# Narrow idle products at the front of TensorE, and a new hand-written order behind them

## The chip, the cores and the metric

The kernel runs on one core of a Trainium2 chip. The metric is the device time of one execution in microseconds (us). TensorE (PE) multiplies, VectorE (DVE) and ScalarE (ACT) do elementwise work, GpSimd (POOL) issues the loads, SyncE (SP) issues the stores. All engines run their own instruction streams in a fixed order and wait for each other by semaphores.

## The reference

Attention with a sliding window of 64 tokens over 8 batches, 8 heads, 576 tokens and head size 64, then a two-layer block with SiLU between the layers:

```
scores = scale * q @ k.T ; mask = (0 <= i - j) & (i - j < 64)
attn = softmax(where(mask, scores, -1e9)) ; a = attn @ v
x = a as (4608 tokens, 512)
h = x @ w_in            # 512 x 2048
out = (h * sigmoid(h)) @ w_out   # 2048 x 512, float32
```

## The kernel before

**Tiles.** The 4608 tokens go in nine tiles of 512 (eight blocks of 64 tokens each). For each tile a "visit" makes the attention of its blocks, for heads 0-3 and for heads 4-7 apart. A visit is: scores on PE (L292; for the very first visits a mask is added by products with `ident`, L285), four exponentials on ACT (L307), a mask product on DVE (L314, not for the first visits), the values product on PE (L323), a reciprocal and a scaling on DVE (L334, L338), and a block transpose on DVE into `xt`, the tile of x (L442). Then come the two layers on PE. Tile 0 does them plainly (L450 and L464, SiLU at L461). Tiles 1 to 8 use a seven-product scheme for 2x2 blocks (L507 and L519), with sums of weights (`wsum`, L469) and of tokens (`xsum`, L485/L487; `gsum`, L493/L496) on DVE, joins on DVE (L526) and copies on ACT (L523).

**The first tile.** It is visited in two halves of 256 tokens. I call the four groups A1 and A2 (heads 0-3, first and second 256 tokens) and B1 and B2 (heads 4-7). Their scores stand on PE in the order A1, A2, B1, B2, their values in the order A1, B1, A2, B2. Each group's scores need q and k of its four heads, loaded by POOL (L224, one load for q and one for k of four heads) and turned by DVE (L255 for k, L258 for q). Values need v, loaded by POOL (L235) and copied half a tile up or down by DVE or ACT (L273, L275). The first layer begins with eight "half products" (4 matmuls each), which use the first 256 tokens alone: four of them read the rows of `xt` from heads 0-3, four those from heads 4-7.

**What sets the order.** `Plan.run` walks the table `ORDER`. A word such as `166P2506` says that step 166 goes to PE and takes the PSUM banks 2, 5, 0 and 6; the letters A, D, G and S stand for ACT, DVE, POOL and SP. So the table fixes the order on each engine, which of ACT and DVE does a copy, and the order in which POOL issues its loads. Eight POOL loads can be under way at a time, and their data come in the order of issue.

**Idle products.** `warm` (L895) multiplies a tile of zeros, `fill`, into a PSUM bank that nobody reads. The plan makes 90 such steps (67 to 156), each 512 columns wide. Of these the table places 36: 24 before the first scores, 7 between A2's and B1's scores, 4 between B2's scores and A1's values, and 1 among the first half products. Steps of this kind that the table doesn't place are left out.

Of the kernel before, what the change touches and what calls it, by code (L numbers as in the profile page):

```python
# [29 lines left out]
class Plan:  # L30
# [88 lines left out]
def kernel(ctx, tc, q, k, v, w_in, w_out, out):  # L119
# [774 lines left out]
    def warm(op_bank):  # L894
        nc.tensor.matmul(banks[op_bank.idx][:, 0:FILL], lhsT=fill[:, 0:128], rhs=fill[:, 0:FILL], start=True, stop=True)  # L895
# [92 lines left out]
```

## Time and profile before

| | us |
|---|---|
| median of 3 runs | 277.21 |
| lowest, highest | 275.41, 277.24 |
| the profiled execution | 276.81 |
| its span, first to last instruction | 275.0 |
| PE busy in the span | 264.7 |
| DVE, ACT, POOL busy | 214.0, 195.6, 129.7 |

The span is what the instruction records cover; the 1.8 us between it and the profiled execution's own time lie around the records and take no part in the argument. PE is busy nearly all the time, but its idle products count as busy too. The DMA engines are close to full until about 185 us.

### The profile page before, as it was taken

The page shows a single profiled execution, that of the slowest core. Times are in us where ns is not written, and L with a number is a line of the kernel's source. Part 1 is how long each engine was busy: PE and PEld are TensorE (multiplying, and loading weights), DVE is VectorE, ACT ScalarE, POOL GpSimd, SP SyncE. Part 2 cuts the span into 40 slices and gives each one's busy share as a digit, 9 for nine tenths or more (in the row PEclk, how much of TensorE's full clock was granted, in tenths as well). Part 3 has the DMA queues.
Part 4 walks back from the last instruction along what each step waited for, and adds up shares of the span by engine and source line. Part 5 has one row for each costly group of instructions (what it writes and reads, how often), then busy time and mean ns, then how long its engine had stood idle before and what let it go on. Part 6 is the DMA issues. An engine that isn't in the chain of part 4 may idle for free.

```text
span 275.0 us, 10018 instructions
## 1 busy us (share of the span) xinstructions
PE 264.7 (96%) x4335; PEld 218.0 (79%) x4342; DVE 214.0 (78%) x426; ACT 195.6 (71%) x361; POOL 129.7 (47%) x194
## 2 busy tenths in 40 slices
PE   7978999999999999999999999999999999999993
PEld 2557844688888888888888888888888888888882
DVE  3757578999996898889799999988867967824741
ACT  1555993699749993987499958893888489537910
POOL 7944566988959758596387335940000000000000
PEclk9999999999999999999999999999999999999999
DMA  6999999999999959999979998990400040003004
GB/s 106 167 190 210 198 191 172 144 198 157 118 151 209 127 56 97 242 122 87 93 179 159 83 126 122 136 121 2 155 0 2 6 155 0 2 29 127 0 2 157
DMA packets 101631, 31.62 MB, mean 115 GB/s; under 512 B 92368, under 2 KB 95440, under 8 KB 101584
## 3 DMA queue, kind: packets, MB, share of 16 engines
q0 software_dynamic: 96128, 21.51, 86.1%
q1 hardware_dynamic: 5456, 9.44, 9.7%
q8 instruction: 35, 0.57, 0.9%
q14 instruction: 12, 0.10, 0.1%
HBM read 42.99 MB, written 9.44 MB: 191 GB/s over the span
## 4 chain that ended last, share of the span: by engine, by line
PE 88%; ACT 4%; DVE 4%; issue 1%; ACTq 0%
PE room L519 36%; PE room L507 35%; PE room L292 4%; PE room L323 4%; PE room L450 4%; PE room L895 4%; PE room L464 2%; ACT es L307 2%; DVE o L338 1%; ACT L307 1%; ACT g L461 1%; DVE es L314 1%; DVE xt L442 1%; PE room L285 1%; ACT L461 0%
## 5 line engine op out<-in xcount | busy, mean ns | idle before, releaser
L529 ACT ACTIVATE g<-room 128x512 bf16<-128x512 f32 x96 | 53.6, 605 | 4.5 <-PE room L507 4.1
L507 PEld LDWEIGHTS <-wsum 128*128 128x128 bf16 x512 | 49.9, 98 | 7.2 <-issue 1.0
L519 PEld LDWEIGHTS <-gsum 128*128 128x128 bf16 x512 | 49.1, 98 | 6.2 <-DVE gsum L496 0.2
L507 PE MATMUL room<-xsum,wsum 128*128 128x256 bf16 x384 | 53.3, 272 | 0.5 <-ACT es L307 0.3
L307 ACT ACTIVATE es<-room 128x512 bf16<-128x512 f32 (+1 forms) x88 | 39.1, 533 | 14.2 <-PE room L292 9.6
L519 PE MATMUL room<-wsum,gsum 128*128 128x256 bf16 x384 | 48.4, 273 | 0.0
L507 PEld LDWEIGHTS <-w_in_sb 128*128 128x128 bf16 x384 | 37.2, 98 | 4.7
L519 PEld LDWEIGHTS <-g 128*128 128x128 bf16 x384 | 36.7, 98 | 4.6
L526 DVE TENSOR_TENSOR room<-room,part 128x512 f32<-128x512 f32 (+1 forms) x41 | 27.8, 684 | 13.7 <-ACT part L523 3.5
L227 POOL DMA_DIRECT2D nat<-in_k_dram x48 | 30.0, 631 | 15.1 <-DVE kT L265 11.4
L507 PE MATMUL room<-xt,w_in_sb 128*128 128x256 bf16 x256 | 36.8, 273 | 0.0
L519 PE MATMUL room<-w_out_sb,g 128*128 128x256 bf16 x256 | 35.7, 273 | 0.0
L227 POOL DMA_DIRECT2D nat<-in_q_dram x48 | 29.9, 637 | 9.7 <-DVE qT L268 6.1
L523 ACT COPY ot<-room 128x512 f32<-128x512 f32 (+1 forms) x23 | 13.3, 582 | 28.6 <-PE room L519 21.5
L235 POOL DMA_DIRECT2D vv<-in_v_dram x32 | 29.6, 940 | 5.0 <-DMA nat<-in_k_dram 1.7
L523 ACT COPY room<-room 128x512 f32<-128x512 f32 x40 | 23.3, 592 | 12.1 <-PE room L507 10.8
L526 DVE TENSOR_TENSOR fin<-room,part 128x512 f32<-128x512 f32 x32 | 21.6, 683 | 9.0 <-PE room L507 6.1
L523 ACT COPY part<-room 128x512 f32<-128x512 f32 x40 | 23.6, 598 | 6.4 <-PE room L519 3.2
L241 POOL DMA_DIRECT2D vv<-in_v_dram x24 | 22.3, 934 | 12.0 <-PE room L323 11.5
L314 DVE TENSOR_TENSOR es<-es,strip 128x1024 bf16<-128x1024 bf16 (+1 forms) x36 | 21.9, 626 | 6.7 <-ACT es L307 6.4
L338 DVE TENSOR_TENSOR o<-room,recips 128x896 bf16<-128x896 f32 (+2 forms) x36 | 25.9, 726 | 0.8
L496 DVE TENSOR_TENSOR gsum<-g,gsum 128x512 bf16<-128x512 bf16 x64 | 25.1, 415 | 0.4
(75 smaller groups left out, 376.8 us busy)
## 6 DMA issues: line engine op xcount, KB each, us to landing
out_dram<-ot SPq DMA_DIRECT2D x16, 512.0 KB, 3.9
vv<-in_v_dram POOLq DMA_DIRECT2D x56, 128.0 KB, 5.0
nat<-in_k_dram POOLq DMA_DIRECT2D x48, 72.0 KB, 4.0
nat<-in_q_dram POOLq DMA_DIRECT2D x48, 72.0 KB, 3.7
w_in_sb<-in_moe_w_in_dram POOLq DMA_DIRECT2D x8, 256.0 KB, 9.2
w_out_sb<-in_moe_w_out_dram POOLq DMA_DIRECT2D x8, 256.0 KB, 9.0
nat<-in_k_dram POOLq DMA_DIRECT2D x4, 288.0 KB, 8.0
nat<-in_q_dram POOLq DMA_DIRECT2D x4, 288.0 KB, 8.2
```

Of the source, the lines that this page charges most:

```text
L227: queue[e].dma_start(out=nats[b % 2][a][kk][32 * h:32 * h + 32].rearrange("p (n x) -> p n x", n=NB), in_=(q, k)[kk][b, 4 * a + h].rearrang ...
L235: queue[e].dma_start(out=vv[b % 2][:, :, 2 * g + 1, 0:D], in_=v[b, :, 128 * g:128 * g + 128].rearrange("h p d -> p h d"))
L241: queue[e].dma_start(out=vv[b % 2][:, :, 2 * g, 0:D], in_=v[b, :, 128 * g - 64:128 * g + 64].rearrange("h p d -> p h d"))
L307: nc.scalar.activation(out=es_part(a, blocks)[:, h], in_=banks[bank.idx][:, 0:64 * n], func=ACTF.Exp, scale=scale)
L314: nc.vector.tensor_mul(t, t, strip[:, s:s + n].rearrange("k n i -> k (n i)").unsqueeze(1).to_broadcast([128, 2, 64 * n]))
L338: nc.vector.tensor_mul(out, at_values(bank, n)[:, :, :, 0:D], recips[:, w:w + 2 * n].rearrange("k (t n) -> k t n", t=bank.wide).unsqueeze( ...
L496: nc.vector.tensor_sub(out=dst[2 * i - 1], in0=g(1, 2 - i), in1=dst[i - 1])
L507: nc.tensor.matmul(banks[bank.idx][:, 256 * i:256 * i + 256], lhsT=lhs(z, i), rhs=rhs(z), start=(start and i == 0 and z == 0), stop=(z == ...
L519: nc.tensor.matmul(banks[bank.idx][:, 256 * m:256 * m + 256], lhsT=lhs(m, i), rhs=rhs(i), start=(start and i == 0 and m == 0), stop=(stop ...
L523: copies[e](out=dst, in_=src)
L526: nc.vector.tensor_add(out=dst, in0=bank, in1=part)
L529: nc.scalar.activation(out=g_tile(pair, 256 * t, 256 * t + 256), in_=src.rearrange("k (f t) -> k f t", f=2), func=ACTF.Silu)
```

## The change

The plan gets 48 further idle steps (1643 to 1690) of 128 columns, and `warm` gets the width as an argument. The table `ORDER` is replaced as a whole. In the new table 17 wide and 19 narrow idle products stand in front of the first scores, mostly in turn, and none anywhere else: the 12 wide ones behind A2's scores are left out. All real steps of the old table stand in the new one, but their order differs on PE, DVE, ACT and POOL through the whole program, and 13 copies change between DVE and ACT (6 go from DVE to ACT, 7 from ACT to DVE).

```
-    "1D 9G 2D 74P7 3D 11G 69P2 72P5 13G 67P0 15G 68P1 73P6 5G 70P3 71P4 19G 7D 78P3 81P6 82P7 86P3 6G 10D 77P2 89P6 90P7 75P0 17G 76P1 80P5 12D 83P0 79P4 "
+    "1D 11G 3D 1643P7 81P6 9G 2D 1644P7 80P5 1645P7 71P4 15G 1646P7 78P3 1647P7 17G 1648P7 89P6 1649P7 1650P7 5G 79P4 1651P7 77P2 1652P7 75P0 6G 1653P7 7D "
...
-    def warm(op_bank):
-        nc.tensor.matmul(banks[op_bank.idx][:, 0:FILL], lhsT=fill[:, 0:128], rhs=fill[:, 0:FILL], start=True, stop=True)
+    def warm(op_bank, n):
+        nc.tensor.matmul(banks[op_bank.idx][:, 0:n], lhsT=fill[:, 0:128], rhs=fill[:, 0:n], start=True, stop=True)
...
-        p.add({"PE": 0.427 * FILL / 512 if i < 4096 / FILL else 0.235 * FILL / 512}, lambda _, wb=wb: warm(wb), [c_fill], 1e6 + i, take=[wb], give=[wb], gate=lambda: first_moe[0]["at"] is None, tag="fill", ins=2)
+        p.add({"PE": 0.427 * FILL / 512 if i < 4096 / FILL else 0.235 * FILL / 512}, lambda _, wb=wb: warm(wb, FILL), [c_fill], 1e6 + i, take=[wb], give=[wb], gate=lambda: first_moe[0]["at"] is None, tag="fill", ins=2)
...
+    for i in range(48):
+        wb = Bank("part")
+        p.add({"PE": 0.107 if i < 32 else 0.06}, lambda _, wb=wb: warm(wb, 128), [c_fill], 2e6 + i, take=[wb], give=[wb], gate=lambda: first_moe[0]["at"] is None, tag="fill", ins=2)
     p.run(ORDER)
```

POOL at its start, before: `nat_87` and `nat_89` are the k of heads 0-3 and 4-7, `nat_86` and `nat_88` their q, `strip` is the mask.

```order
L224 DMA nat_87<-in_k_dram 128x1152
L224 DMA nat_86<-in_q_dram 128x1152
L224 DMA nat_89<-in_k_dram 128x1152
L224 DMA nat_88<-in_q_dram 128x1152
L184 MEMSET strip 128x64
L185 ISA
L185 AFFINE_SELECT strip<-strip 128x64
L187 AFFINE_SELECT strip<-strip 128x64
L235 DMA vv_98<-in_v_dram 128x8x64
```

And POOL at its start now:

```order
L224 DMA nat_86<-in_q_dram 128x1152
L224 DMA nat_87<-in_k_dram 128x1152
L224 DMA nat_88<-in_q_dram 128x1152
L235 DMA vv_98<-in_v_dram 128x8x64
L184 MEMSET strip 128x64
L185 ISA
L185 AFFINE_SELECT strip<-strip 128x64
L187 AFFINE_SELECT strip<-strip 128x64
L191 MEMSET ident 128x128
L192 AFFINE_SELECT ident<-ident 128x128
L193 AFFINE_SELECT ident<-ident 128x128
L224 DMA nat_89<-in_k_dram 128x1152
```

The k of heads 4-7 moved from the third place among the loads to the fifth, behind the first load of v and behind the making of the mask and the identity.

DVE from the first write into `xt_75` (tile 0 of x) to the last, before: `o_100` holds the attention of heads 0-3, `o_101` that of heads 4-7.

```order
L442 STREAM_TRANSPOSE xt_75<-o_100 128x4x2x32
L334 RECIPROCAL recips<-room 128x8
L338 TENSOR_TENSOR o_101<-room,recips 128x2x256
L442 STREAM_TRANSPOSE xt_75<-o_101 128x4x2x32
L945 MEMSET good 128x1
L334 RECIPROCAL recips<-room 128x8 x2
L338 TENSOR_TENSOR o_100<-room,recips 128x2x256
L442 STREAM_TRANSPOSE xt_75<-o_100 128x4x2x32
L338 TENSOR_TENSOR o_101<-room,recips 128x2x256
L442 STREAM_TRANSPOSE xt_75<-o_101 128x4x2x32
```

And now:

```order
L442 STREAM_TRANSPOSE xt_75<-o_100 128x4x2x32
L273 COPY vv_98<-vv_98 64x8x64
L334 RECIPROCAL recips<-room 128x8
L338 TENSOR_TENSOR o_101<-room,recips 128x2x256
L334 RECIPROCAL recips<-room 128x8
L442 STREAM_TRANSPOSE xt_75<-o_101 128x4x2x32
L334 RECIPROCAL recips<-room 128x8
L338 TENSOR_TENSOR o_101<-room,recips 128x2x256
L338 TENSOR_TENSOR o_100<-room,recips 128x2x256
L442 STREAM_TRANSPOSE xt_75<-o_101 128x4x2x32
L442 STREAM_TRANSPOSE xt_75<-o_100 128x4x2x32
```

A copy of v came in from ACT, and of the second halves heads 4-7 (B2) are now turned ahead of heads 0-3 (A2).

118 rows, old and new, of the table ORDER are left out of this document.

## The prediction

> **What bounds the kernel now.** I read the page first, then the busy time by stretches, then the timeline of each engine over the first 32 us.
>
> ```profile
> span 275.0 us, 10018 instructions
> PE 264.7 (96%) x4335; PEld 218.0 (79%) x4342; DVE 214.0 (78%) x426; ACT 195.6 (71%) x361; POOL 129.7 (47%) x194
> PE room L519 36%; PE room L507 35%; PE room L292 4%; PE room L323 4%; PE room L450 4%; PE room L895 4%; PE room L464 2%; ACT es L307 2%; DVE o L338 1%; ACT L307 1%; ACT g L461 1%; DVE es L314 1%; DVE xt L442 1%; PE room L285 1%; ACT L461 0%
> ```
>
> The chain of waits is PE's second and first layers (L519, L507) for seven tenths of the span. The stretches show where PE is not full (start and end, length, then each engine's busy us):
>
> ```profile
> 17.20:22.40 5.20, 4.23 (x109) 3.25 (x110) 3.84 (x10) 1.44 (x3) 2.33 (x4) 1.00 1.22 209
> 34.10:52.40 18.30, 17.31 (x287) 8.37 (x291) 15.26 (x39) 11.86 (x26) 12.81 (x21) 1.00 1.43 163
> 52.40:60.00 7.60, 7.60 (x70) 6.61 (x69) 7.57 (x16) 7.57 (x15) 6.76 (x11) 1.00 1.36 212
> 60.00:270.00 210.00, 209.31 (x3518) 182.59 (x3516) 170.84 (x330) 157.17 (x284) 88.04 (x124) 1.00 0.89 97
> 270.00:275.00 5.00, 0.36 (x4) 0.08 (x1) 0.65 (x1) 0.37 (x1) 0.00 (x0) 1.00 0.38 125
> ```
>
> From 60 to 270 us PE is idle for 0.7 us in 210. The real products are the same in both kernels, so this stretch can hardly shrink, and the time is set by when PE becomes full and by the 5 us of end. What there is to win lies ahead of 52 us. PE's timeline there (start, length, work, and in brackets the idle time before it):
>
> ```profile
> 1.39 7.60 PE L895 MATMUL room<-fill 128*128 128x512 bf16 x24 [1.39 <-DVE fill L213]
> 8.82 0.60 PE L285 MATMUL room<-block,ident 128*128 128x256 bf16 x4
> ...
> 10.60 1.79 PE L895 MATMUL room<-fill 128*128 128x512 bf16 x6
> 12.23 0.60 PE L285 MATMUL room<-block,ident 128*128 128x256 bf16 x4
> ...
> 13.10 0.61 PE L285 MATMUL room<-block,ident 128*128 128x256 bf16 x4
> ...
> 14.00 1.04 PE L895 MATMUL room<-fill 128*128 128x512 bf16 x4
> 14.96 0.67 PE L323 MATMUL room<-vv,es 128*32 128x65 bf16 x44
> 17.21 0.60 PE L323 MATMUL room<-vv,es 128*32 128x65 bf16 x52 [1.58 <-issue]
> 17.74 1.26 PE L450 MATMUL room<-xt,w_in_sb 128*128 128x256 bf16 x8
> 18.93 0.43 PE L323 MATMUL room<-vv,es 128*32 128x65 bf16 x32
> ...
> 21.32 0.60 PE L450 MATMUL room<-xt,w_in_sb 128*128 128x256 bf16 x4 [0.43 <-DVE xt L442]
> 22.42 7.91 PE L450 MATMUL room<-xt,w_in_sb 128*128 128x256 bf16 x71 [0.51 <-DVE xt L442]
> ```
>
> Three holes stand here that no idle product fills: 1.58 us in the middle of B1's values, for which the profile shows no releaser, and 0.43 and 0.51 us for writes into `xt`.
>
> **The change, part by part.** All sums are against the profiled execution, 276.81 us with a span of 275.0. It lies 0.40 under the median of the three runs, 277.21, and inside their spread.
>
> *1. The narrow products at the front.* The wide ones by their two speeds:
>
> ```profile
> 1.39:5.97 4.58, 4.58 (x11) 1.63 (x12) 1.00 0.72 122
> 5.97:8.82 2.85, 2.85 (x14) 1.18 (x12) 1.00 1.09 196
> ```
>
> Eleven take 4.58 us (0.42 each), the other thirteen 2.85 (0.22 each): the clock doubles at about 6 us. Now it is 17 x 512 + 19 x 128 = 11136 columns for 24 x 512 = 12288. The first 4.58 us pass 11 x 512 = 5632 columns; the other 5504 at 0.22 per 512 need 2.4, so the products end at 8.4 instead of 8.82. If each of the 12 further weight loads (0.1 us by the rows above, 1.18 / 12) came on top, they would end at 9.6. The first scores also need q and k turned:
>
> ```profile
> 7.06 1.21 DVE L258 STREAM_TRANSPOSE qT<-nat 128x576 f32<-128x576 f32 x1 [0.22 <-DMA nat<-in_q_dram]
> 8.48 1.26 DVE L255 STREAM_TRANSPOSE kT<-nat 128x576 f32<-128x576 f32 x1 [0.21 <-DMA nat<-in_k_dram]
> 11.86 0.29 DVE L273 COPY vv<-vv 64x512 bf16<-64x512 bf16 x1 [0.74 <-DMA vv<-in_v_dram]
> ```
>
> A1's pair is turned by 8.27. I take 8.4 for A1's start, and 0.4 us sooner for A1 and A2. Nothing of it reaches B1, as the next part shows.
>
> *2. Twelve products left out, k of heads 4-7 later, ACT in another order.*
>
> ```profile
> 9.83 2.32 ACT L307 ACTIVATE es<-room 128x256 bf16<-128x256 f32 x8 [7.61 <-PE room L292]
> 12.17 0.62 ACT L273 COPY vv<-vv 64x512 bf16<-64x512 bf16 x1
> 12.80 0.62 ACT L275 COPY vv<-vv 64x512 bf16<-64x512 bf16 x1
> 13.32 2.29 ACT L307 ACTIVATE es<-room 128x256 bf16<-128x256 f32 x8
> 15.64 0.62 ACT L273 COPY vv<-vv 64x512 bf16<-64x512 bf16 x1
> ```
>
> Eleven of the twelve lie beside these exponentials: B1's scores take over banks of A1 and A2, which come free at 12.15, and began at 12.23. Leaving the seven out gains under 0.1 us. Now ACT begins with an exponential of A2, so at 8.4 + 1.8 = 10.2 (A1 and A2 together took 8.82 to 10.60). B1 waits for seven of them, 0.29 each: 12.3. Its k now lands fifth: the third load was down at 8.46 (its turn began at 8.48), a load of v takes about 1.0 (by the copy at 11.86, which waited for the second of them, behind a fourth load down at about 9.9), one of k or q 1.4 (7.06 to 8.48), so 10.9, and it is turned by 12.2. So B1 starts at 12.4 with no idle products before it, where it started at 12.23 with them.
>
> B2's scores now wait for the last exponential of A2, which stands behind the first of B1: 13.3 + 2 x 0.3 = 13.9 (before 13.10). A1's values follow B2's scores, 0.9 us later, at 14.9; they began at 14.96. So the four left out there gain nothing. The last exponential that B1's values need comes after eight steps of ACT from 13.35, seven exponentials and one copy: 16.0. ACT's last v copy ends at 16.0 + 2 x 0.29 + 0.62 = 17.2, which lets A2's values start at 17.3; they ran right behind the hole that ends at 17.21. Sum of this part: 0.0, bounds -0.3 and +0.8 (if k lands after another load).
>
> *3. The hole at 15.6.* Its row has no releaser. PE's instructions come by DMA:
>
> ```profile
> q8 instruction: 35, 0.57, 0.9%
> ```
>
> 0.57 MB in 35 packets are 16 KB each. PE's 4335 + 4342 instructions share them, 66 bytes each, so a packet holds some 250. Before the hole stand 35 idle products, 144 of scores and 44 of values, with a weight load each: 446 instructions, while the loads keep the DMA engines full. I read the hole as PE waiting for its next instructions. [...]
>
> 36 idle products stand ahead of B1's values now, so the hole stays at that place. I let it end 0.4 us sooner, as the instructions behind A1 begin 0.4 sooner: 16.8. B1's values end near 17.1 (before, their reciprocal began at 17.67). By part 2 A2's values start at 17.3 anyway, so this gains no time of PE, but DVE starts B1's reciprocal at 17.2.
>
> *4. The waits for `xt` and the idle product among the half products.* DVE:
>
> ```profile
> 17.67 0.21 DVE L334 RECIPROCAL recips<-room 128x8 f32<-128x8 f32 x1 [0.68 <-PE room L323]
> 17.91 0.73 DVE L338 TENSOR_TENSOR o<-room,recips 128x512 bf16<-128x512 f32 x1
> 18.68 0.45 DVE L442 STREAM_TRANSPOSE xt<-o 128x256 f32<-128x256 f32 x1
> ...
> 20.82 0.45 DVE L442 STREAM_TRANSPOSE xt<-o 128x256 f32<-128x256 f32 x1 [0.55 <-PE room L450]
> 21.19 0.70 DVE L338 TENSOR_TENSOR o<-room,recips 128x512 bf16<-128x512 f32 x1
> 21.92 0.45 DVE L442 STREAM_TRANSPOSE xt<-o 128x256 f32<-128x256 f32 x1
> ```
>
> A2's turn waited for PE (0.55), and then half products waited for it, though they read other columns: a write into `xt` and the half products around it in the table wait for each other if they share rows of x. So the order decides. Now DVE does: copy 0.3, reciprocal and scaling of B1, reciprocal of A2, turn of B1, reciprocal and scaling of B2, scaling of A2, turn of B2, turn of A2. From 17.2, with 0.2, 0.7 and 0.45 per step: B1 turned at 18.8, B2 at 20.85, A2 at 21.3. On PE from 17.3: two values groups (0.43 each) and eight half products of four matmuls, 7.91 / 71 = 0.11 each, so 0.87 + 3.5 us. The sixth reads rows of heads 4-7 and stands behind B2's turn: it would start at 20.4 and waits until 20.9, 0.4 us. The eight end at 22.1. Before, 25 of their 32 matmuls were done at 22.42, the rest by 22.42 + 7 x 0.11 = 23.2. **Gain 1.1 us**, made of the two waits (0.94) and the idle product (0.22) against a new wait of 0.4 and an earlier start by a quarter of a microsecond. If the hole ends as late as before, DVE is 0.4 later and the gain 0.7; with no wait it is 1.5.
>
> *5. From there to 60 us.* The loads come in the same number and at the same pace, DVE and ACT have the same work but for copies that change sides. In 52.4 to 60 DVE is full, 7.57 of 7.60: a lead of PE alone would end there. DVE's chain starts from tile 1's values, which PE makes, so most of the lead passes on. I keep 1.0 of 1.1, bounds 0 and 1.5 + 1.0 (all the idle time of 34 to 52, 18.30 - 17.31, gone too).
>
> *6. The rest, 60 to 270 us.* The waits of PE there:
>
> ```profile
> PE room L507 <- ACT es L307: 0.3, 1, 0.3
> PE room L323 <- DVE o L338: 0.2, 1, 0.2
> PE room L507 <- issue: 0.2, 1, 0.2
> ```
>
> At most 0.7 can be won. The order is new on all engines and its waits are in no trace. The nearest rows are these 0.3 and 0.2 per wait: two more, half offset by those that go, cost 0.2; that is what I take. The far end is such a wait in each of 14 large visits, 14 x 0.3 = 4.2. The end behind 270 us keeps its stores: 0.
>
> Sum: 276.81 - 1.0 + 0.2 = **276.0 us**.
>
> **The rivals.**
>
> *A: the lead is lost in the stretch where DVE is full*, and nothing else changes: 276.81 + 0.2 = 277.0. For it speaks 7.57 of 7.60; against it that DVE's steps are fed by PE.
>
> *B: the clock falls back.* Without the twelve products PE does 4 x 0.9 us of scores and 0.4 of values from 8.4 to 16.0 and nothing else. If it slows down, it needs again the 4.58 us of work that the front took, at half speed: 4.58 / 2 = 2.3 us lost behind 17.3, and 276.0 + 2.3 = 278.3, slower than before. It decides from the first idle stretch that is long enough. In this trace 1.58 us idle did not do it: the matmuls behind ran at 0.11. My longest stretch is 2.1 us (10.2 to 12.3). [...]
>
> *C: the new order waits in the steady part*: exponentials that free a score bank too late for PE, once in each of 14 large visits, 0.3 each: 276.0 + 4.2 = 280.2, slower. It decides at three such waits, where the gain is gone. For it: DVE is busy for 170.84 and ACT for 157.17 of the 210 us, so a step that moves has little room. Against it: before has one.
>
> *D: the holes go altogether*: the instruction hole (1.58), both waits (0.94) and the idle product (0.22) vanish: 276.81 - 2.74 = 274.1. Against it the exponentials of part 2 and the full DMA engines. [...]
>
> *E: the change does nothing*: the idle products were never on the path, and the rest cancels: 276.8.
>
> **How the numbers follow.** About 1% is what a measurement of this kernel can tell from no change: 274.4 to 280.0 around the median. Forecast 0.42, A 0.13, E 0.07, B 0.10, C 0.17, D 0.11. Of B all but a tenth of its mass stays inside 1%; of C, whose waits may be longer than 0.3, I count everything above; unnamed mishaps of the new order take some of the forecast's mass, 0.05. So slower by over 1%: 0.17 + 0.01 + 0.05 = 0.23; faster by over 1%: D and a little, 0.12; same 0.65. The range leaves out a tenth on each side: 274.3 to 280.3.
>
> **What would show it.** In the new profile: L895 once at the front, ending near 8.4; the second L285 group near 12.4 and B1's values with a hole of about 0.8 us marked "issue"; one wait of L450 on `xt`, not two, and the eight half products done at 22.1; PE full from 52 us on as before, with 0.7 to 1.2 us idle between 60 and 270. Matmuls of 0.22 us at L450 would mean B. Many rows "L507 <- es" or "L519 <- DVE" would mean C. No "issue" row near 16 us would mean D. The forecast is wrong if the first layer's start doesn't move, or if PE idles over 3 us behind 60 us.

## The result and the profile after

The changed kernel took 278.81 us (median of nine runs, 277.76 to 279.10), the kernel before 277.06 beside it (nine runs, 275.41 to 278.29): a ratio of 1.0061, interval 1.0038 to 1.0083. A gain of 0.3% was forecast and a loss of 0.6% came. The loss is smaller than the 1% named in the prediction, but the interval leaves no doubt of its sign. Ratios and intervals here leave out the few runs that the chip made in a slower state, and they are not simply quotients of the medians.

The profiled execution took 278.73 us, 1.92 more than that of before. Its page: the span, the engines' busy time, PE's granted clock in 40 slices, and the chain of waits:

```profile
span 277.0 us, 10005 instructions
...
PE 263.5 (95%) x4337; PEld 218.8 (79%) x4342; DVE 213.3 (77%) x427; ACT 193.8 (70%) x360; POOL 129.6 (47%) x194
...
PEclk9959999999999999999999999999999999999998
...
PE room L519 35%; PE room L507 35%; PE room L450 6%; PE room L464 5%; PE room L292 4%; PE room L323 4%; DMA nat<-in_k_dram 2%; ACT es L307 1%; DVE o L338 1%; POOL nat L224 1%; DVE es L314 0%; DVE kT L255 0%; ACT ot L523 0%; POOL vv L235 0%;
```

Two things are new. PE's granted clock has a 5 in the third of 40 slices, and the load of k stands in the chain. PE's timeline of the front shows both (start, length, work, and in brackets the idle time before it):

```profile
1.39 6.48 PE L895 MATMUL room<-fill 128*128 128x128 bf16 x36 [1.39 <-DVE fill L213]
7.70 0.60 PE L285 MATMUL room<-block,ident 128*128 128x256 bf16 x4
...
10.50 0.54 PE L285 MATMUL room<-block,ident 128*128 128x256 bf16 x2 [0.76 <-ACT es L307]
11.32 0.27 PE L285 MATMUL room<-block,ident 128*128 128x256 bf16 x1 [0.28 <-ACT es L307]
11.88 0.27 PE L285 MATMUL room<-block,ident 128*128 128x256 bf16 x1 [0.28 <-ACT es L307]
13.39 0.42 PE L292 MATMUL room<-qT,kT 32*128 32x64 bf16 x32 [1.24 <-DVE kT L255]
...
15.43 0.68 PE L323 MATMUL room<-vv,es 128*32 128x65 bf16 x34
16.58 0.62 PE L323 MATMUL room<-vv,es 128*32 128x65 bf16 x30 [0.47 <-ACT es L307]
18.02 0.63 PE L323 MATMUL room<-vv,es 128*32 128x65 bf16 x32 [0.81 <-DVE vv L273]
18.58 1.03 PE L450 MATMUL room<-xt,w_in_sb 128*128 128x256 bf16 x4
19.55 0.63 PE L323 MATMUL room<-vv,es 128*32 128x65 bf16 x32
20.11 10.98 PE L450 MATMUL room<-xt,w_in_sb 128*128 128x256 bf16 x92
```

The first row of L450 is the forecast's own test for rival B: four matmuls of the half products take 1.03 us where four of before took 0.60. The same rows show that the hole without a releaser has gone from B1's values (the 30 matmuls at 16.58 wait for exponentials), and that none of the half products waits for `xt`.

The clock changes of the trace lie 3.41 us, or a multiple of it, apart: here at 4.64, 14.88 and 21.70. So I cut the busy time into these stretches (start and end, length, PE, weight loads, DVE, ACT, POOL, the granted clock, DMA share, GB/s):

```profile
4.64:8.05 3.41, 3.41 (x27) 1.99 (x25) 2.57 (x4) 0.00 (x0) 3.26 (x7) 1.00 1.16 193
8.05:11.46 3.41, 2.23 (x74) 1.29 (x72) 1.84 (x4) 1.67 (x7) 3.41 (x6) 1.00 1.68 159
11.46:14.88 3.42, 1.46 (x38) 0.61 (x37) 2.44 (x6) 1.39 (x6) 2.27 (x4) 1.00 1.61 152
14.88:18.29 3.41, 2.12 (x120) 1.71 (x123) 2.01 (x7) 3.34 (x9) 1.96 (x3) 0.50 1.31 201
18.29:21.70 3.41, 3.41 (x71) 2.25 (x60) 2.52 (x6) 0.71 (x1) 1.11 (x2) 0.50 1.23 206
```

After a stretch in which PE was busy for 1.46 of 3.42 us the clock halves, and it comes back after one that PE filled. There was no idle stretch of 3.41 us; the longest single wait behind the first scores is 1.24.

The steady part in the same view:

```profile
60.00:270.00 210.00, 208.97 (x3515) 182.51 (x3513) 171.08 (x329) 155.34 (x283) 87.60 (x123) 1.00 0.88 95
```

PE is busy for 208.97 us there, against 209.31. At the end of the program, the five stores (L533: least, median and longest ns, then first and last start). Of before:

```profile
L533 SPq DMA_DIRECT2D out_dram<-ot x5: 345/418/691, 267.8 to 271.5; - x5
```

And of the changed kernel:

```profile
L533 SPq DMA_DIRECT2D out_dram<-ot x5: 372/421/544, 271.1 to 273.1; - x5
```

PE's last products, of before and then of after:

```profile
269.76 0.60 PE L519 MATMUL room<-w_out_sb,gsum 128*128 128x256 bf16 x4
```

```profile
270.41 0.60 PE L519 MATMUL room<-w_out_sb,gsum 128*128 128x256 bf16 x4
```

PE ends at 270.36 before and 271.01 now. From there to the end of the span it was 4.7 us and is 5.9. So of the 1.92 us about 1.3 lie behind PE's last product and 0.65 ahead of it. Matching the products of the two traces one by one splits the 0.65: PE is 0.75 us behind when the half products are done, only 0.31 behind by 52 us, and 0.8 behind again by 90 us, after this row and a wait of 0.36 us for a copy at 83.67:

```profile
80.86 0.59 PE L292 MATMUL room<-qT,kT 32*128 32x64 bf16 x53 [0.36 <-issue]
```

So there were three suspects: the end, the clock, and a hole at 80 us.

### The profile page after: what moved, and what is told of

It reads as the page before. It is cut to its first block, busy times and chain, and to the rows that moved or that the text cites. A ratio compares the mean times of both kernels' runs of the same rounds, so it can differ in the third digit from the quotient of the medians.

```text
span 277.0 us, 10005 instructions
## 1 busy us (share of the span) xinstructions
PE 263.5 (95%) x4337; PEld 218.8 (79%) x4342; DVE 213.3 (77%) x427; ACT 193.8 (70%) x360; POOL 129.6 (47%) x194
## 4 chain that ended last, share of the span: by engine, by line
PE 89%; DMA 2%; DVE 2%; ACT 2%; POOL 1%; issue 1%; ACTq 0%; DVEq 0%; POOLq 0%
PE room L519 35%; PE room L507 35%; PE room L450 6%; PE room L464 5%; PE room L292 4%; PE room L323 4%; DMA nat<-in_k_dram 2%; ACT es L307 1%; DVE o L338 1%; POOL nat L224 1%; DVE es L314 0%; DVE kT L255 0%; ACT ot L523 0%; POOL vv L235 0%; ACT room L523 0%
## 5 line engine op out<-in xcount | busy, mean ns | idle before, releaser
L235 POOL DMA_DIRECT2D vv<-in_v_dram x32 | 29.4, 928 | 13.9 <-PE room L507 9.6
L523 ACT COPY part<-room 128x512 f32<-128x512 f32 x40 | 23.7, 599 | 7.5 <-PE room L507 4.3
L338 DVE TENSOR_TENSOR o<-room,recips 128x128 bf16<-128x128 f32 (+2 forms) x36 | 25.8, 727 | 0.7
L493 DVE TENSOR_TENSOR gsum<-g 128x1024 bf16<-128x1024 bf16 x32 | 21.6, 684 | 3.5 <-ACT g L529 3.4
```

The costliest lines, as they stand in the source:

```text
L235: queue[e].dma_start(out=vv[b % 2][:, :, 2 * g + 1, 0:D], in_=v[b, :, 128 * g:128 * g + 128].rearrange("h p d -> p h d"))
L338: nc.vector.tensor_mul(out, at_values(bank, n)[:, :, :, 0:D], recips[:, w:w + 2 * n].rearrange("k (t n) -> k t n", t=bank.wide).unsqueeze( ...
L493: nc.vector.tensor_sub(out=gsum[:, u, 0:4:2], in0=gall[:, lo:hi + 1, :, 256:512], in1=gall[:, lo].rearrange("k f (t n) -> k t f n", t=2))
L523: copies[e](out=dst, in_=src)
```

## The experiments

Three series, each on one chip with its own runs of the kernel before, whose medians there were 276.22, 276.50 and 276.65. "PE's end" and "clock halved for" are from the profiled execution of each, the second from the first full clock to PE's end; for the kernel before they were 270.36 and 0.

| kernel | median | ratio and interval | PE's end | clock halved for |
|---|---|---|---|---|
| changed, copy 1627 earlier (`t1_copy`) | 277.93 | 1.0064 (1.0043 to 1.0085) | 271.74 | 10.2 us |
| changed, end of before (`t2_tail`) | 277.52 | 1.0075 (1.0045 to 1.0105) | 270.89 | 10.2 us |
| changed, 17 wide idle products added (`c1_fills`) | 278.61 | 1.0094 (1.0064 to 1.0124) | 271.70 | 0 |
| the same with the end of before (`c2_both`) | 277.81 | 1.0074 (1.0046 to 1.0101) | 271.08 | 0 |
| before, idle products as changed (`b1_edit`) | 276.80 | 1.0031 (1.0005 to 1.0056) | 269.84 | 6.8 us |
| before, the twelve left out (`b1_nofill`) | 277.80 | 1.0022 (0.9990 to 1.0054) | 273.08 | 6.8 us |
| before, end as changed (`b2_tail`) | 278.08 | 1.0051 (1.0023 to 1.0079) | 272.59 | 3.4 us |
| changed, idle products and end of before (`c3_wide`) | 276.63 | 1.0015 (0.9991 to 1.0040) | 269.72 | 0 |
| changed kernel again (`after2`) | 279.31 | 1.0100 (1.0063 to 1.0137) | 272.21 | 10.2 us |
| changed, idle products of before (`c3_late`) | 277.73 | 1.0048 (1.0029 to 1.0067) | 270.10 | 0 |
| `c3_wide` again (`c3_again`) | 276.39 | 1.0003 (0.9977 to 1.0030) | 269.23 | 0 |
| before, narrow front and six of the twelve (`b4_six`) | 276.70 | 1.0015 (0.9994 to 1.0037) | 270.40 | 3.4 us |

### The end: the copy or the place of the stores

```
-1607P 1619P 1616P 1623P 1624P 1625P 1617P 1626P 1629A 1620P 1627A 1628D
+1607P 1627A 1619P 1616P 1623P 1624P 1625P 1617P 1626P 1629A 1620P 1628D
```

> The changed kernel, with one step of ACT moved: the output copy 1627, ready with product 1607, stands ahead of copy 1629 again, which waits for product 1617. The five stores keep their place in the table, behind the last copy 1630. Theory 1 (the late copy holds all stores): the first store starts near 268.3 instead of 271.1, and the span falls by 1.2 us, to about 275.8. Theory 2 (a store waits for every write into ot that stands ahead of it in the table): the first store still starts near 271.1, and the time stays at 278.8.

This moves one copy on ScalarE and leaves the stores at the end of the table. The second kernel restores the whole end (1629 on DVE again, the stores between the products):

```
-1624P 1625P 1617P 1626P 1629A 1620P 1627A 1628D 1621P 1630A 1631S 1632S 1633S 1634S 1635S
+1631S 1624P 1632S 1625P 1617P 1629D 1626P 1633S 1620P 1628D 1621P 1630A 1634S 1635S
```

> The changed kernel, with the whole tail as before: copy 1629 on DVE, copy 1627 early, and the first three stores in the table right behind the writes that they need. Both theories of the tail: five stores begin near 268.4, the last lies after PE's end by 4.7 us instead of 6.0, so 1.3 less: about 277.5. If the tail is only noise of one execution: 278.8.

SyncE's stores in the kernel with the one copy moved:

```profile
269.59 3.65 SPq L533 DMA_DIRECT2D out_dram<-ot  x5
```

And in the changed kernel:

```profile
271.06 2.56 SPq L533 DMA_DIRECT2D out_dram<-ot  x5
```

ScalarE's last copies, of before and then of the changed kernel, where copies 1629, 1627 and 1630 run in one row:

```profile
267.17 0.58 ACT L523 COPY ot<-room 128x512 f32<-128x512 f32 x1 [3.61 <-PE room L519]
270.40 0.37 ACT L523 COPY ot<-room 128x256 f32<-128x256 f32 x1 [2.65 <-PE room L519]
```

```profile
270.17 1.25 ACT L523 COPY ot<-room 128x256 f32<-128x256 f32 x3 [5.96 <-PE room L519]
```

The one copy is enough: PE's end to the span's end is 4.76 us with it and 4.74 with the whole end restored, against 5.95. So the place of the store words makes 0.02 us. What costs is that copy 1627 stands behind 1629, which waits for products that end near 270.15, and that its output is the first of five stores, which SyncE starts about 0.5 us apart (271.1 to 273.1). With the first store at 271.06, the last is issued at 273.1, 2.1 us behind PE's end; before it was 1.1. The ratios, 1.0064 and 1.0075, don't show the gain against the 1.0061 of the changed kernel. That kernel had no run in this series, and its clock was halved for 6.8 us in its profile and for 10.2 us in these two; the pairs below have the price in medians.

The end alone, put into the kernel before:

```
-1622D 1615P 1627A 1618P 1616P 1623P 1631S 1624P 1632S 1619P 1617P 1625P 1629D 1626P 1633S 1620P 1628D 1621P 1630A
+1622D 1615P 1618P 1616P 1623P 1624P 1619P 1617P 1625P 1629A 1626P 1620P 1627A 1628D 1621P 1630A 1631S 1632S 1633S
```

> The kernel before with the end of the changed one: copy 1629 on ScalarE ahead of copy 1627, all five stores issued at the end. Theory (the late copy and its 512 KB store are 1.2 us of the loss, and nothing else of the order matters for them): PE's end to the span's end grows from 4.7 to 5.9 us, the run is 1.0 to 1.4 us longer. Rival (the tail is late only because everything ahead of it is late): no change, within 0.2 us.

PE's end to the span's end grew to 5.83 us and the ratio is 1.0051, as the theory has it. This kernel's program up to 260 us is that of the kernel before, and yet its profiled PE ended 2.2 us later. Its front:

```profile
14.61 0.67 PE L325 MATMUL room<-vv,es 128*32 128x65 bf16 x44
17.77 0.60 PE L325 MATMUL room<-vv,es 128*32 128x65 bf16 x52 [2.49 <-issue]
```

(L325 is L323 of the kernel before.) The hole of 1.58 us is 2.49 here, and the stretch around it, 15.49 to 18.90, has PE busy for 1.13 of 3.41 us; the clock fell for one stretch. So executions with the same front differ by 2 us there, and one profile against another tells less than medians do.

### The idle products: put back into the changed kernel

```
-176A 160A 177A 31G
+176A 160A 91P4 92P2 93P4 94P2 95P4 96P2 97P4 98P2 99P4 100P2 101P4 102P2 103P4 104P2 177A 31G
...
-171P2 188A
+171P2 105P6 106P6 107P6 188A
```

> The changed kernel with idle products put back: 14 wide ones between A2's and B1's scores, 3 behind B1's values. Both theories: the granted clock stays at 1.0 from 5 us to the end of PE's work, and the first eight half products end near 22.4 instead of 24.1. Theory 1 (the half clock costs the kernel what it costs the front): 1.5 us less, 277.3. Theory 2 (tile 1 waits for DVE and loads anyway, and takes up most of the lag, as it fell from 0.75 to 0.3 by 46 us): 0.3 less or nothing, 278.5.

> The changed kernel with the tail as before and the 17 idle products of c1_fills. The parts add up: by theory 1 of the clock 278.8 - 1.3 - 1.5 = 276.0, by theory 2 278.8 - 1.3 - 0.3 = 277.2, level with the kernel before.

The clock stayed at 1.0 in both, so the missing idle products are what let it fall. This holds beyond the profiles: the mean clock is 0.996 or more in all twelve runs of these two kernels, and 0.976 to 0.984 in all fifteen of the changed one. The times did not get better: 278.61 is near theory 2 and 277.81 is above both theories, and the half products ended at 23.8 and 23.7, not at 22.4. Placed like this, the idle products hold the clock and gain no time. With the end restored PE was 0.35 us behind at the half products, level with the kernel before (within 0.2 us) from 47 to 79 us, and then lost a whole microsecond by 90 us, most of it at one place:

```profile
77.99 1.26 PE L519 MATMUL room<-wsum,g 128*128 128x256 bf16 x10
80.10 0.83 PE L519 MATMUL room<-wsum,g 128*128 128x256 bf16 x6 [0.85 <-issue]
```

No semaphore releases it, and it stands in the middle of a step. Counted in PE's weight loads, of which the traces have every one, it stands at number 1248 in both kernels, and so do the 0.36 us of the changed kernel, in another step. The hole of the kernel before at B1's values stands at number 225, as do those of `b1_nofill`, `b2_tail` and `b4_six`. (With the matmuls these are numbers near 2490 and 448 of PE's instructions.)

The packets of the instruction queue (q8 in the prediction) fit. In all fourteen traces every pause of 0.2 us or more at these two places ends 2.2 to 2.6 us after the start of a packet of 16 KB (of before, 14.86 and 17.21; of the changed kernel at 80 us, 78.39 and 80.86), and PE passed without one only where it came there 2.2 us or more after that start. No row says for which engine a packet is.

### The order alone

If the place is fixed in the instruction stream, fewer idle products ahead of it put later work there. `c3_wide` has 24 wide idle products at the front, 10 behind A2's scores and 2 behind B1's values, 36 as in the kernel before, and the end of before.

```
-1643P7 81P6 ... 1644P7 80P5 1645P7 71P4 ...
+74P7 69P2 ... 72P5 67P0 ...
...
-176A 160A 177A 31G
+176A 160A 91P4 93P2 92P4 97P2 94P4 95P2 96P4 99P2 100P4 98P2 177A 31G
...
-171P2 188A
+171P2 102P6 101P6 188A
```

> The changed kernel with 36 wide idle products as in the kernel before (24 at the front, 10 behind A2's scores, 2 behind B1's values) and the end of the kernel before; so its order alone is new. PE has 34 instructions fewer ahead of 80 us than in the run with 36 + 17 idle products, which had a hole of 1.2 us in the middle of L519 there. Theory F (the hole is PE waiting for its next block of instructions, at a fixed place in the instruction stream): the hole stands at the same instruction number, about 2490, and is 0.2 to 0.6 us; clock 1.0 throughout; PE 0 to 0.2 us behind the kernel before at 79 us and 0.3 to 0.6 behind at the end. Rival G (the order's loads or exponentials around 80 us make it): 1.0 us of hole at the same products, 0.8 us or more behind at the end.

The hole at 80 us went from 0.85 to about 0.2 us, hidden in one row (64 products of scores, L294 = L292 of before):

```profile
79.25 0.91 PE L294 MATMUL room<-qT,kT 32*128 32x64 bf16 x64
```

They take 0.68 us elsewhere, and the pause stands at weight load 1248 again. In the second profile of the same kernel there is none. So the new order does not make the hole by itself, and theory F has the place and the clock right. It has the lag wrong: PE ended 0.64 us ahead of the kernel before, not 0.3 to 0.6 behind. The medians show no such lead: with the clock and the end restored the new order costs and gains nothing that they can tell, 1.0015 and, again, 1.0003.

### The idle products taken out of the kernel before

Idle products as in the changed kernel, all else as before:

```
-74P7 3D 11G 69P2 72P5 13G 67P0 ...
+1643P7 81P6 3D 11G 1644P7 80P5 1645P7 13G 71P4 ...
...
-160A 91P0 161A 30G 16D 159A 93P2 176A 92P1 31G 178A 97P4 179A 94P0 177A 95P3 32G 25A 96P1 ...
+160A 161A 30G 16D 159A 176A 31G 178A 179A 177A 32G 25A ...
```

> The kernel before, its order kept in everything but the idle products: 19 narrow and 17 wide ones at the front, the twelve behind A2's scores left out. Theory P (the missing idle products let the clock fall, whatever the order): the granted clock drops to 0.5 somewhere between 12 and 25 us, PE is 0.4 to 1.3 us behind the kernel before after the eight half products, and most of it is taken up by 50 us, so the run is 0.1 to 0.5 us longer. Rival Q (the clock falls only because the new order has longer waits of PE between 9 and 16 us): the clock stays at 1.0 and the run is within 0.2 us. Rival R (the idle products are the whole loss): 1.5 to 2 us longer.

And the second half of this edit alone:

> The kernel before without its twelve idle products behind A2's scores, front of 24 wide ones kept. Theory P: the clock falls as in the run without them and with the narrow front (0.5 for 5 to 10 us), 0.1 to 0.5 us longer. Rival Q: the clock stays at 1.0, within 0.2 us. Rival N (the narrow front is what matters): the clock stays here and falls in the other.

The clock fell in both profiles, by theory P: with the narrow front at 11.34 us, with the wide one at 16.43, for 6.8 us each. Rivals Q and N are out. So neither the narrow products nor the new order is needed for it. It does not fall every time: of the ten runs of `b1_nofill` that its ratio counts, four have a mean clock of 1.000 and took 274.99 to 276.13 us, and six have 0.985 to 0.998 and took 277.34 to 279.05. Even with the twelve in place it is 0.990 or less in three such runs of the kernel before, out of 78 (277.71, 278.57 and 278.99).

The cost by the ratios, 0.9 and 0.6 us, is above the expected 0.1 to 0.5, though both intervals reach into that and the second still holds 1.0. The lag misses the expectation too, and the profiles lie on both sides of it: `b1_edit` has no hole at the front at all and PE was 0.4 us ahead of before behind the half products and 0.5 at its end; `b1_nofill` had a hole of 2.2 us at weight load 225, was 2.8 behind at the half products, and took up only 0.1 of that by 50 us. A long hole empties a stretch (in `b2_tail` 2.49 us of hole, 1.13 of 3.41 us busy) and so may cost both the clock and the time; the runs do not part the two.

### One series for the sum

The changed kernel as it is:

> The changed kernel once more, beside the three that follow. Theory S (the loss is a sum: late copy and stores at the end 1.2 us, missing idle products and the half clock they allow 0.3 to 1.0 us, the new order of the steady part about 0): 1.0055 to 1.0085 of the kernel before. In the trace the granted clock is 0.5 for a multiple of 3.41 us, after a stretch of 3.41 us in which PE was busy for less than about 62% of it; where the clock stays at 1.0, no such stretch was under 62%.

The kernel of the section on the order, with the end of the changed kernel (the first diff of the experiments and the second, read backwards):

> The changed kernel with the 36 wide idle products of the kernel before, but with its own late end. By theory S only the end is left: 1.003 to 1.006 of the kernel before, 0.8 to 1.4 us above the run with the old end, 5.9 us from PE's end to the span's end, clock 1.0 up to 270 us. Rival T (the end costs nothing that a median shows): within 0.3 us of the run with the old end.

And that kernel itself:

> The changed kernel's order with the 36 wide idle products and the end of the kernel before, a second time. Theory S: 0.999 to 1.003 of the kernel before. If the order of the steady part costs something of its own, 1.004 or more.

The medians add up: 276.39 with the order alone (before 276.65), 277.73 with the late end too, 279.31 with the idle products changed as well. So the end costs 1.3 us and the idle products 1.6 here, the latter uncertain by about 1 us, for `after2` has six runs between 277.97 and 280.50. Its ratio, 1.0100, lies above the expected 1.0055 to 1.0085; those of `c3_late` and `c3_again` are as expected. In its first measurement the changed kernel was at 1.0061, which leaves only 0.4 for them. Its two profiles show why this part is not one number: the clock was halved for 6.8 us in the first, and PE 0.75 us behind at the half products; in the second 10.2 us and 1.9.

The expectation's 62% was too sharp. The stretches of all profiles, by the share that PE was busy:

| | share of the stretch | clock in the next |
|---|---|---|
| `b2_tail`, `after`, `after2` | 0.33, 0.43, 0.49 | halved |
| `b1_nofill`, `b1_edit` | 0.56, 0.58 | halved |
| `b4_six`, `t1_copy`, `t2_tail` | 0.60, 0.61, 0.64 | halved |
| `c3_late`, `b1_nofill` | 0.60, 0.62 | stays 1.0 |
| `c3_wide`, `c3_again`, `after`, before | 0.65, 0.65, 0.66, 0.69 | stays 1.0 |
| `c1_fills`, `c2_both` | 0.73, 0.75 | stays 1.0 |

The two rows that fix the lower edge, of the order with the old idle products and the late end, and of the kernel before without the twelve:

```profile
15.79:19.21 3.42, 2.05 (x97) 1.19 (x86) 2.91 (x8) 3.38 (x8) 1.69 (x3) 1.00 1.25 203
```

```profile
13.02:16.43 3.41, 1.92 (x110) 1.24 (x93) 1.72 (x5) 3.37 (x11) 1.49 (x4) 1.00 1.13 169
16.43:19.84 3.41, 1.82 (x47) 1.42 (x47) 1.77 (x6) 1.20 (x1) 1.19 (x3) 0.50 1.23 202
```

With PE busy for 2.05 of 3.42 us the first kept its clock, with 1.92 of 3.41 the second lost it. These shares rest on modelled ends of matmuls, and the edge lies at 0.60 to 0.65 in these runs. The longest wait within the stretch does not sort them: `b4_six`, `b1_nofill` and `t2_tail` lost the clock with none over 0.76 us, and before kept it with one of 1.00.

### Six idle products instead of twelve

The front of the changed kernel in the kernel before, and the first six of the twelve kept, where PE waits for the exponentials ahead of B1's scores (1.31 us in `b1_edit`):

```
+ ... 160A 91P0 161A 30G 16D 159A 93P2 176A 92P1 31G 178A 97P4 179A 94P0 177A 95P3 32G ...
```

> The kernel before with 19 narrow and 17 wide idle products at its front, and of the twelve behind A2's scores only the first six, which fill PE's wait for B1's k. In the same kernel without the six the clock fell at 11.3 us, after a stretch in which PE was busy for 58%; with them that stretch is busy for over 90%. Theory W (the clock is set by how much of a stretch of 3.41 us PE is busy, not by one long wait, and these six are enough): 1.0 up to 270 us, PE 1.0 to 1.6 us ahead of the kernel before behind the half products, 0.5 to 1.2 ahead at its end; 0.996 to 0.999 of the kernel before. It falls if the stretch from about 14.8 us, with fewer idle products than the kernel before, goes under 62%: then 1.001 to 1.004.

The stretch ahead was filled as expected (98%), but the one from 12.89 to 16.31 went to 60%, by the wait ahead of A1's values and a hole of 0.5 us at weight load 225, and the clock fell for 3.4 us. That is the case named at the end of the expectation, with its price: 1.0015. No version here beats the kernel before by more than its interval.

## Why the prediction was wrong

Against the forecast of 276.0 the profiled execution is 2.7 us longer. At 60 us PE is 0.3 behind where 1.0 ahead was forecast; 0.1 more was lost from there to PE's end than the 0.2 of the sum; and 1.3 lie in the end, forecast 0. Two steps failed: the missing idle products were put at nothing, since rival B's condition for the clock to fall was wrong, and so was the order at the end.

*1, the front.* Right: the narrow products end at 7.9, forecast 8.4, and bring nothing.

*2, B1's k.* The price of the new order of loads was too low. The k of heads 4-7 was forecast down at 10.9 and DVE began its turn at 12.07:

```profile
12.07 1.26 DVE L255 STREAM_TRANSPOSE kT<-nat 128x576 f32<-128x576 f32 x1 [1.97 <-DMA nat<-in_k_dram]
```

POOL issued it at 5.72, behind the mask and the identity, 6.3 us ahead; I had spaced the loads by their landings and left that out. That the late issue is the cause is argued: no run moves it. B1's mask products ran ahead of k (10.50), and its scores came at 13.39, about half a microsecond after the forecast (12.4 and 0.5 of mask products); A1's values at 15.43 (forecast 14.9), A2's at 18.02 (17.3). "Leaving the seven out gains under 0.1 us" is right; that it costs nothing is not: with the idle products of before in this order (`c3_wide`, `c3_again`, `c3_late`) the clock holds in the profiles, and its mean is 0.991 or more in all 36 runs.

*3, the hole.* Right as to what it is, as far as the runs show: it stands at the same weight load, 225, in kernels with 24, 36 and 42 idle products, which put different work there. Wrong as to what becomes of it: that place is reached about 1 us later than before, and the packet ahead of it started at 12.79 us instead of 14.86: PE came there at 16.6, 3.8 us after that start, and did not pause. The missing "issue" row was named as the sign of rival D, and D did not come: the waits for exponentials and for v kept A2's values at 18.02. Of a program's 35 packets few can be seen in a pause: the trace of before has five waits of PE marked "issue", 2.3 us in all, 1.58 of them here, and that of the changed kernel five, 1.1 us in all, none of them here. At the two places 0 to 2.5 us showed while the DMA engines were full (in the DMA row of before every slice from 12 to 19 us is a 9).

*4, the half products.* The mechanism was right where the clock held. `c3_again` has one wait for `xt`, as forecast (0.4):

```profile
21.23 4.96 PE L452 MATMUL room<-xt,w_in_sb 128*128 128x256 bf16 x44 [0.17 <-DVE xt L444]
```

(L452 is L450 of before.) Its half products were done at 22.6, where before's were done at 23.3 and the forecast has 22.1; `c3_wide` and `c3_late` had 0.24 us of lead there, and the four profiles with the changed idle products were 0.75 to 1.93 behind. So up to 0.75 of the 1.1 us came true with the old idle products and none without them.

*Rival B* is what happened at the front, and 0.10 was too little for it. The failing sentence is "It decides from the first idle stretch that is long enough": by the table of the stretches, what decides is the busy share of a stretch of 3.41 us, not the length of one wait. The busy times in the forecast itself, 4 x 0.9 + 0.4 us between 8.4 and 16.0, would have given 53% and spoken for it. No stretch had to be empty: the clock fell after ones with PE busy for 0.33 to 0.64 of 3.41 us. B's price, 2.3 us, was too high by the medians: 0.4 to 1.6 were measured for the idle products with all that hangs on them. In the first halved stretch PE waits for 1.29 of 3.41 us, for exponentials (0.47) and for v (0.81), so no more than the other 2.12 us ran at the half clock. The 0.44 us that the changed kernel makes up between the half products and 52 us are no part of this: the kernels of the new order whose clock held make up the same 0.44 there (`c2_both` from 0.35 behind to 0.10 ahead, `c3_again` from 0.75 ahead to 1.20).

*5 and 6, the steady part.* PE's waits there are now:

```profile
PE room L507 <- ACT room L523: 0.4, 1, 0.4
PE room L292 <- issue: 0.4, 1, 0.4
PE room L507 <- issue: 0.2, 1, 0.2
```

Two new ones against two that went, as the sum had it, and PE's busy time between 60 and 270 us fell by 0.34 for a forecast of 0.2. That is in part luck: one of the two is the hole at 80 us, which the forecast did not have there. Rival C is out: the order alone measures 1.0015 and 1.0003.

*The end.* "The end behind 270 us keeps its stores: 0" is the other step that failed, and the one that cost most of the 1.9 us. The stores are the same, but the order in front of the first of them is not, and the last 1.3 us of the loss are there. The end of the table was in the diff; I had read it for PE only.

So the 1.9 us of the two profiles are 1.3 at the end, and for the rest the front (the halved clock, k's late load) and the hole at 80 us. The end is shown by three pairs of kernels (`c1_fills` and `c2_both`, `c3_late` and `c3_again`, before and `b2_tail`: 0.8, 1.3 and 1.6 us between medians), that the clock follows the idle products by the trace of every kernel, and their price by the third series' medians. How much of the idle products' 0.4 to 1.6 us is the halved clock itself, and how much the hole that comes and goes beside it, stays open. That the holes are PE's instruction fetch is inferred from their fixed numbers and from the packets ahead of them; no row shows a releaser.

## What to carry to other kernels

The idle products were worth 0.4 to 1.6 us here, with what they do for the clock: before leaving any out, read from the kernel's own trace how far apart its clock changes lie (3.41 us in these) and add up PE's busy time in each such stretch around them. Here the clock stayed after shares of 0.65 and more and fell after those under 0.60; between the two it did either. In a hand-written order look at the last dozen words of every queue, not only TensorE's: here the first of a row of five stores set the end, and one copy in front of it cost 1.2 us (PE's end to the span's end 5.95 against 4.76). And compare medians within one series, for two profiles of the same front differed by 2 us.

## What the runs showed of the hardware

- In these fourteen traces the clock changes in stretches of 3.41 us on a grid that differs from run to run (first full clock at 4.5 to 6.9 us). It fell after PE was busy for 33 to 64% of one and stayed after 60% and more. It came back after stretches of 98% and 100%, once after 83%, and did not after 82% and 84%.
- In the same traces PE paused for 0 to 2.5 us at two places, its weight loads 225 and 1248, whatever work stood there, while the DMA engines were full (a 9 in the DMA row of before from 12 to 19 us). The pauses of 0.2 us and more ended 2.2 to 2.6 us after an instruction packet of 16 KB started (before: 14.86 and 17.21).
- SyncE started the changed kernel's five stores about 0.5 us apart (271.1 to 273.1, the last copy into `ot` ended at 271.4), so the last of them started 2 us behind the first.
